# Grouped attention with a one-headed key beside an MLP: the output projection's products spread over a step, the first scores issued among the MLP's last products, and the row-sum test moved ahead of the last products

## The chip, the core and the metric

The kernel runs on one core of one Trainium2 chip. The metric is the device time of one execution in microseconds (us); of several runs the median is taken. Engines: TensorE (PE; its weight loads are PEld), VectorE (DVE), ScalarE (ACT), GpSimd (POOL) and SyncE (SP, which here only issues DMAs and waits). A queue of an engine that holds waits, branches and DMA issues carries a q behind the engine's name (SPq, PEldq).

## The reference

Input x has 2048 rows of 448. With xn = layernorm(x), the result is the sum of x, an attention and an MLP:

```
q = (xn @ wq) in 16 heads of 28;  k = xn @ wk;  v = xn @ wv      (one k and one v for all heads)
scores = q k^T * 28**-0.5;  p = softmax(scores);  attention = (p v, heads side by side) @ wo
h = gelu(layernorm(xn) @ w1 + b1);  mlp = h @ w2 + b2            (w1: 448 x 1792, w2: 1792 x 448)
out = x + attention + mlp
```

All is float32.

## The kernel before

The rows are cut into 4 chunks of 512. The program has four stages. The first normalizes x, transposes it and projects q, k and v; q goes to DRAM. The second is the MLP, in 56 slots (4 chunks by 14 column tiles of 128): `mlp1` multiplies by w1 (11 matmuls) and hands the result to ACT, DVE and POOL for the gelu and for a split in a high and a low part (`hh`, `hl`); `mlp2`, two slots later, multiplies both by w2 (12 matmuls) into four PSUM banks `m2`. After a chunk's last slot DVE adds the four banks to the rows (L596), which go back to DRAM. The last two `mlp2` slots stand by themselves, since no `mlp1` is left.

The third stage is attention, over 16 units (4 row chunks by 4 groups of 4 heads), unit u of 8 steps. A step issues 8 score matmuls (L700, for two key tiles and four heads), each into one of six PSUM banks; ACT turns each bank into weights by one exponential (L702). Behind the 8 scores stand the products of weights and values (`pv`, L709) for the scores of the step before, into the bank `po`; they are 8 in the program and 16 in the trace. The weights are not shifted by their true row maximum but by an estimate from a sample of the keys (`find_max`, once a unit: a matmul L536 into the bank `mo`, then DVE L537, L538, L542, L543). A column of ones in v gives the row sums. A fourth part, at the end, tests the row sums (`bad`, `count`): if one is outside of two limits, all of attention is done again with the true maximum. That code stands in the program behind a branch (L800) and is not run with these inputs.

Between the scores of a step stand side jobs of earlier units. Three matter here:

- `norm_jobs` of a finished unit: DVE copies `po` (L679), a DMA turns the row sums by 128 partitions (`rc`, L681), DVE stores them and takes the reciprocal (L683, L684), DMAs spread it through DRAM to all partitions (`tr`, L685, L688), DVE multiplies (L690) and splits (`oth` L692, `otl` L693 on POOL).
- `o_parts`: the output projection of a unit, four row tiles A to D, each with three matmuls (L665, L667, L669) that accumulate in `mo`, of which there is only one bank; after the third DVE adds `mo` to the row (L671). The first matmul of the next tile, and the matmul of `find_max`, wait until `mo` has been read.
- loads for the next unit (`load_unit`) and of rows for the next chunk.

A list `PIECES` says how many of the twelve matmuls stand in each of seven steps, 4 to 10 steps behind the end of the unit. Within a step the jobs stand at two places, after the second and after the fifth score; the list of a step's jobs is halved between them, in order of registration. So two matmuls of a step are neighbours where both fall in one half. After the last products `last_norm` (L712) normalizes the last unit, multiplies by wo (L719) and adds the rows (L732); then come the test (L792 to L798), the load of `count` into a register of each engine (L799) and the branch.

Of the kernel before, what the change touches and what calls it, by code (L numbers as in the profile page):

```python
# [10 lines left out]
F32 = mybir.dt.float32  # L11
# [7 lines left out]
P = 128  # L19
# [11 lines left out]
MLP_ORDER = 1, 2, 3, 0  # L31
HD = D // 2
WEIGHTS = 28
PIECES = 2, 1, 2, 1, 2, 2, 2
LIMITS = 0.25, 2.0 ** 40


# [1 line left out]
def block_kernel(ctx, tc, x, wq, wk, wv, wo, w1, b1, w2, b2, out):  # L39
# [511 lines left out]
    def find_max(u):  # L551
        mr = keep.tile([P, CW // 32], F32, name="mr", bufs=2)
        block_max(kd, mr)
        shift_rows(u, mr)

    ph1b = ExitStack()
    hp = ph1b.enter_context(tc.tile_pool(name="hp", bufs=3))
    php = ph1b.enter_context(tc.tile_pool(name="php", bufs=2, space=PSUM))
# [5 lines left out]

    def mlp1(c, ft):
        yh, yl = xts[MLP_ORDER[c], True]
        ph = php.tile([P, CW], F32, name="ph")
# [12 lines left out]
        pool.tensor_sub(hl, hx, f(hh))  # L580
        hs[c, ft] = (hh, hl)

    def mlp2(c, ft):
        if ft == 0:
            m2s[c] = [m2p.tile([P, CW], F32, name=f"m2_{k}")[:, 0:D] for k in range(CT)]
        m2 = m2s[c]
        hh, hl = hs.pop((c, ft))
        terms = ((hh, w2h), (hh, w2l), (hl, w2h))
        for k in range(CT):
            for i, (h, w) in enumerate(terms):  # L590
                pe.matmul(m2[k], h[:, k * P:(k + 1) * P], w[:, ft, :], start=(ft == 0 and i == 0),  # L591
                          stop=(ft == NF - 1 and i == 2))
            if ft == NF - 1:
                t = CT * MLP_ORDER[c] + k
                a = lines.pop(t)
                dve.tensor_add(a, a, m2[k])  # L596
                nc.sync.dma_start(ad[:, t, :], a)

    norms = {}
    mslots = [(c, ft) for c in range(NCH) for ft in range(NF)]  # L600
    for c in range(len(KEPT), NCH):
        g = norm_gen(MLP_ORDER[c], lambda shape: php.tile(shape, F32, name="ph"))
        for i in range(2 * CT + 1):
            norms[NF * (c - 1) + 4 + i] = lambda g=g: next(g, None)
    for n in range(len(mslots) + 2):
        c, ft = mslots[n] if n < len(mslots) else (NCH, n - len(mslots))
        if 3 <= ft < 11 and ft % 2 and len(KEPT) <= c + 1 < NCH:
            line(CT * MLP_ORDER[c + 1] + (ft - 3) // 2)
        k = ft - (10 if c < NCH - 1 else 5)
        if c < NCH and 0 <= k < CT:  # L610
            line(CT * MLP_ORDER[c] + k)
        if c < NCH and 0 < k <= CT:
            a = lines[CT * MLP_ORDER[c] + k - 1]
            pool.tensor_add(a, a, b2b)
# [12 lines left out]
        if n in norms:  # L627
            norms[n]()
        if (c, ft) == (NCH - 1, 7):
            find_max(0)  # L630
        if n >= 2:
# [5 lines left out]
    pr = ctx.enter_context(tc.tile_pool(name="pr", bufs=6, space=PSUM))  # L637
    op = ctx.enter_context(tc.tile_pool(name="op", bufs=1, space=PSUM))

    def weights_tile():  # L640
# [8 lines left out]
    dve.tensor_copy(woh, wor)  # L649
    dve.tensor_sub(wol, wor, f(woh))  # L650

    sums = keep.tile([P, NU, CW // 32], F32, name="sums")
    rows = {}
# [39 lines left out]
        pool.tensor_sub(otl, oc, f(oth))  # L693
        yield

    pos, ps = {}, {}

    def scores(u, kt, j):
        s = pr.tile([P, CW], F32, name="s")
        pe.matmul(s, ks[:, kt * P:(kt + 1) * P], qss[u][:, j, :], start=True, stop=True)  # L700
        p = att.tile([P, CW], F32, name="p", bufs=WEIGHTS)
        act.activation(p, s, AF.Exp, scale=SCALE)  # L702
        ps[u, kt, j] = p

    def pv(u, kt):
        if kt == 0:
# [2 lines left out]
            pe.matmul(pos[u][32 * j:32 * j + 32, :], vs[:, kt, :], ps[u, kt, j],  # L709
                      start=(kt == 0), stop=(kt == NT - 1))  # L710

    def last_norm(u, po):  # L712
# [3 lines left out]
        outs = [pr.tile([P, CW], F32, name="s") for _ in range(CT)]  # L716

        def product(k):
            pe.matmul(outs[k][:, 0:D], on[:, k * P:(k + 1) * P], wor[:, g, :], start=True, stop=True)  # L719

        for i in range(2):
            h, r = slice(256 * i, 256 * i + 256), slice(8 * i, 8 * i + 8)
            dve.transpose(tr[:, h], po[:, h])
            dve.reciprocal(rc[:, r], blocks(tr[:, h])[:, :, 0])
            dve.transpose(blocks(rb[:, h]), rc[:, r, None].to_broadcast([P, 8, 32]))
            dve.tensor_mul(on[:, h], po[:, h], rb[:, h])
            pool.tensor_copy(sums[:, u, r], blocks(tr[:, h])[:, :, 0])
            for k in (2 * i, 2 * i + 1):
                product(k)
        for k in range(CT):  # L730
            a = rows[c, k]
            dve.tensor_add(a, a, outs[k][:, 0:D])  # L732
            (nc.scalar if k % 2 else nc.sync).dma_start(ov[:, CT * c + k, :], a)

    side = {}

    def at(step, job):
        side.setdefault(min(step, PER * NU - 1), []).append(job)

    PER = NT // 2  # L740
    for u in range(NU):
# [6 lines left out]
    todo = [(u, kt, j) for u in range(NU) for kt in range(NT) for j in range(4)]  # L748
    waiting = []

    def weighted():
# [4 lines left out]
        norm = norm_jobs(u, pos.pop(u))  # L756
        next(norm)
        for d in (1, 3):
            at(PER * (u + 1) + d, lambda: next(norm))
        parts = []  # L760

        def part():
# [1 line left out]
                parts.append(o_parts(*units[u]))  # L764
            next(parts[0])

        for d, n in enumerate(PIECES if u < NU - 2 else (3, 3, 3, 3)):
            for _ in range(n):
                at(PER * (u + 1) + 4 + d, part)

    for step in range(PER * NU):
        for i in range(8):
            u, kt, j = todo.pop(0)
            scores(u, kt, j)
            if i in (1, 4):
                jobs = side.pop(step, [])
                if i == 1:
                    half = (len(jobs) + 1) // 2
                    side[step] = jobs[half:]
                    jobs = jobs[:half]  # L780
                for job in jobs:
                    job()
        weighted()
        waiting = [(u, kt - 1), (u, kt)]
    weighted()
    last_norm(NU - 1, pos.pop(NU - 1))

    bad = keep.tile([P, 2], F32, name="bad")
    count = keep.tile([1, 1], I32, name="count")
    bits = sums.rearrange("p u e -> p (u e)").bitcast(I32)  # L790
    lo, hi = (float(int.from_bytes(struct.pack(">f", v), "big")) for v in LIMITS)
    dve.tensor_reduce(bad[:, 0:1], bits, axis=AX.X, op=ALU.max)  # L792
    dve.tensor_reduce(bad[:, 1:2], bits, axis=AX.X, op=ALU.min)
    dve.tensor_scalar(bad[:, 0:1], bad[:, 0:1], hi, 0.0, op0=ALU.is_gt, op1=ALU.add)
    dve.scalar_tensor_tensor(bad[:, 0:1], bad[:, 1:2], lo, bad[:, 0:1], op0=ALU.is_lt, op1=ALU.add)
    pf = bank([1, 1])
    pe.matmul(pf, bad[:, 0:1], one[:, 0:1], start=True, stop=True)
    dve.tensor_copy(count, pf)  # L798
    outside = nc.values_load(count)  # L799
    with tc.If(outside > 0, preferred_fallthrough_block=False):  # L800
# [46 lines left out]
```

## Time and profile before

| what | value |
|---|---|
| three runs | 922.11, 922.5, 923.2 us; median 922.5 |
| the profiled execution | 923.97 us, of which the span from the first to the last instruction is 922.2 |
| granted TensorE clock, mean | 0.995 |
| PE / ACT / DVE busy | 97% / 73% / 32% of the span |
| MLP, first to last second-layer product | 76.5 to 351.8 us |
| attention, first score to last product of weights and values | 352.6 to 909.2 us |
| normalization of the last unit, test, branch, end | 909.2 to 922.2 us |

How it is read: the chain of waits follows back from the last instruction to what released it, and prints start, duration and what ran. A row of the groups or of the timeline gives in brackets, or behind a bar, the idle time of the engine before it and what ended that. Matmuls are pipelined: the next starts before the row of the last ends, so the chain's shares are better to count with than rows of single matmuls.

### The profile page before, as it was taken

What the parts mean: (1) busy time and instruction counts of PE and PEld (TensorE: products, weight loads), DVE (VectorE), ACT (ScalarE), POOL (GpSimd) and SP (SyncE); (2) the same over time, 40 slices, a digit from 0 to 9 for tenths busy, and PEclk for the clock granted to TensorE, in tenths of its full rate; (3) what the DMA queues carried; (4) which work ended last, traced back from release to release, by engine and by line L of the source; (5) the groups of instructions that cost most, each with busy time, mean ns of one, the idle gap of its engine ahead of it and who ended that gap; (6) DMA issues with size and microseconds to landing.
All of it is one profiled execution on the core that took longest, in us unless ns stands there. A gap on an engine that the chain in (4) does not pass through costs nothing.

```text
span 922.2 us, 13010 instructions
## 1 busy us (share of the span) xinstructions
PE 895.0 (97%) x4925; PEld 567.5 (62%) x4925; DVE 292.7 (32%) x551; ACT 676.4 (73%) x1284; POOL 155.4 (17%) x150
## 2 busy tenths in 40 slices
PE   9989999999999999999999999999999999999995
PEld 8867878888888885454454444444444454454442
DVE  7865454344444433012122122112122122121113
ACT  5754443334443337999999999999999999999983
POOL 6443243233234331000000000000000000000000
PEclk9999999999999999999999999999999999999998
DMA  9781112002003104302202312201312202222001
GB/s 298 207 270 40 41 61 80 1 1 80 21 21 96 28 9 125 92 23 63 42 22 53 96 58 55 49 23 53 101 53 53 52 23 53 84 70 53 1 13 44
DMA packets 42046, 60.08 MB, mean 65 GB/s; under 512 B 10794, under 2 KB 26744, under 8 KB 41976
## 3 DMA queue, kind: packets, MB, share of 16 engines
q1 hardware_dynamic: 40568, 58.60, 22.1%
q8 instruction: 41, 0.67, 0.3%
q10 hardware_dynamic: 1408, 0.57, 0.2%
q14 instruction: 29, 0.24, 0.1%
HBM read 43.16 MB, written 14.80 MB: 63 GB/s over the span
## 4 chain that ended last, share of the span: by engine, by line
PE 93%; DVE 3%; ACT 2%; issue 1%; POOL 0%; DMA 0%; ACTq 0%; DVEq 0%; POOLq 0%
PE s L700 29%; PE po L709 26%; PE m L591 14%; PE ph L177 12%; PE qp L177 3%; PE mo L665 2%; PE mo L669 1%; PE mo L667 1%; PE ph L182 1%; PE ph L180 1%; DVE row L671 1%; PE qp L301 1%; DVE hz L574 0%; PE mo L536 0%; DVE hx L576 0%
## 5 line engine op out<-in xcount | busy, mean ns | idle before, releaser
L702 ACT ACTIVATE p<-s 128x512 f32<-128x512 f32 x1024 | 516.0, 627 | 44.6 <-PE s L700 40.8
L700 PE MATMUL s<-xh,ks 128*128 128x512 f32 x1024 | 301.9, 408 | 0.8 <-issue 0.8
L700 PEld LDWEIGHTS s<-xh,ks 128*128 128x128 f32 x1024 | 182.5, 188 | 138.8 <-ACT p L702 110.3
L709 PE MATMUL po<-p,vs 128*32 128x512 f32 x2048 | 246.0, 598 | 0.0
L709 PEld LDWEIGHTS po<-p,vs 128*32 128x32 f32 x2048 | 53.5, 109 | 122.5 <-issue 117.0
L572 ACT ACTIVATE hx<-ph,b1t 128x512 f32<-128x512 f32 x56 | 38.5, 687 | 115.6 <-PE ph L182 105.9
L671 DVE TENSOR_TENSOR row<-row,mo 128x448 f32<-128x448 f32 x60 | 37.3, 621 | 244.8 <-PE mo L669 243.6
L580 POOL TENSOR_TENSOR hl<-hx,hh 128x512 fp32r<-128x512 f32 x56 | 77.5, 1384 | 184.4 <-DVE hh L579 181.7
L693 POOL TENSOR_TENSOR otl<-oc,oth 128x512 fp32r<-128x512 f32 x15 | 19.4, 1292 | 515.9 <-DVE oth L692 466.0
L591 PE MATMUL m<-w2l,hh 128*128 128x448 f32 x224 | 82.5, 369 | 0.9 <-DVE w2l L379 0.9
L591 PE MATMUL m<-w2h,hl 128*128 128x448 f32 x224 | 82.1, 367 | 1.0 <-POOL hl L580 1.0
L591 PE MATMUL m<-w2h,hh 128*128 128x448 f32 x224 | 82.3, 367 | 0.2 <-DVE a L596 0.2
L574 DVE SCALAR_TENSOR_TENSOR hz<-hz,hx 128x512 f32<-128x512 f32 x56 | 45.2, 808 | 106.0 <-ACT hz L573 105.7
L575 ACT ACTIVATE hz<-hz 128x512 f32<-128x512 f32 x56 | 35.4, 632 | 49.4 <-DVE hz L574 49.4
L177 PE MATMUL ph<-xh,w1h 128*128 128x512 f32 x168 | 66.1, 394 | 2.4 <-DVE qe L402 2.4
L177 PE MATMUL ph<-xl,w1h 128*128 128x512 f32 x168 | 66.3, 395 | 0.0
L177 PE MATMUL ph<-xh,w1l 128*128 128x512 f32 x168 | 66.2, 394 | 0.0
L576 DVE SCALAR_TENSOR_TENSOR hx<-hz,hx 128x512 f32<-128x512 f32 x56 | 39.1, 698 | 43.2 <-ACT hz L575 43.2
L679 DVE COPY oc<-po 128x512 f32<-128x512 f32 x15 | 10.4, 692 | 119.1 <-PE po L709 119.1
L591 PEld LDWEIGHTS m<-w2l,hh 128*128 128x128 f32 x224 | 42.1, 188 | 7.4 <-DVE w2l L379 3.3
L591 PEld LDWEIGHTS m<-w2h,hh 128*128 128x128 f32 x224 | 42.1, 188 | 5.5 <-DVE a L596 0.6
L591 PEld LDWEIGHTS m<-w2h,hl 128*128 128x128 f32 x224 | 42.1, 188 | 4.9 <-POOL hl L580 1.6
(148 smaller groups left out, 758.9 us busy)
## 6 DMA issues: line engine op xcount, KB each, us to landing
xh<-qd SPq DMA_DIRECT2D x64, 224.0 KB
qd<-qe SPq DMA_DIRECT2D x24, 256.0 KB
a<-in_A_x_dram SPq DMA_DIRECT2D x24, 224.0 KB
tr<-ld SPq DMA_DIRECT2D x60, 64.0 KB
ad<-a SPq DMA_DIRECT2D x16, 224.0 KB
qm<-qd SPq DMA_DIRECT2D x64, 56.0 KB
row<-ad SPq DMA_DIRECT2D x16, 224.0 KB
raw<-in_B_w_dram SPq DMA_DIRECT2D x7, 448.0 KB
```

Of the source, the lines that this page charges most:

```text
L177: pe.matmul(ps, w, v, start=(n == 0), stop=False)
L572: act.activation(hx, ph, AF.Identity, bias=b1t[:, ft:ft + 1])
L574: dve.scalar_tensor_tensor(hz, hz, 1.0, hx, op0=ALU.add, op1=ALU.mult)
L575: act.activation(hz, hz, AF.Tanh, scale=GELU[1])
L576: dve.scalar_tensor_tensor(hx, hz, 1.0, hx, op0=ALU.add, op1=ALU.mult)
L580: pool.tensor_sub(hl, hx, f(hh))
L591: pe.matmul(m2[k], h[:, k * P:(k + 1) * P], w[:, ft, :], start=(ft == 0 and i == 0), stop=(ft == NF - 1 and i == 2))
L671: dve.tensor_add(a, a, po)
L693: pool.tensor_sub(otl, oc, f(oth))
L700: pe.matmul(s, ks[:, kt * P:(kt + 1) * P], qss[u][:, j, :], start=True, stop=True)
L702: act.activation(p, s, AF.Exp, scale=SCALE)
L709: pe.matmul(pos[u][32 * j:32 * j + 32, :], vs[:, kt, :], ps[u, kt, j], start=(kt == 0), stop=(kt == NT - 1))
```

## The change

Five edits:

1. Side jobs get a slot of their own (`at(step, job, slot)`): the two or one matmuls of the output projection that a step holds stand after the second and the sixth score (three: also after the eighth), `norm_jobs` after the fourth, all else after the fifth. The counts of a step stay.
2. The six score banks are now two pools of three, `ring_a` and `ring_b`, used in turn. `ring_a` exists from the MLP on, whose `mlp1` uses it too (three banks in place of two). So in the MLP's last two slots `mlp2` issues one score after each three products, eight in all; their weights go into two free `xl` buffers. Step 0 then issues no scores.
3. The split of wo on DVE (`split_out`) moves from ahead of attention to step 3.
4. The row sums of the first 15 units are reduced ahead of the last products (`worst`); for the last unit the test stands inside `last_norm`, ahead of the reciprocal of the second half, and the two copies of sums on POOL go. One of the four last rows is added by ACT and POOL in place of DVE.
5. `mark_branch_hint_location("outside", hint="LikelyTaken")` stands ahead of `last_norm`, and the branch's preferred fallthrough is the code that does attention again, in place of the short block that skips it.

```
-PIECES = 2, 1, 2, 1, 2, 2, 2
+EARLY = 8
+PARTS = 2, 1, 2, 1, 2, 2, 2
...
+    ring_a = ctx.enter_context(tc.tile_pool(name="ra", bufs=3, space=PSUM))
...
+            if then is not None:
+                then()
...
+    def scores(u, kt, j):
+        s = score_bank()
+        pe.matmul(s, ks[:, kt * P:(kt + 1) * P], qss[u][:, j, :], start=True, stop=True)
+        p = early.pop(0) if early else att.tile([P, CW], F32, name="p", bufs=WEIGHTS)
+        act.activation(p, s, AF.Exp, scale=SCALE)
...
+        if n >= len(mslots):
+            t = f(xl_p.tile([P, 4, CW], F32R, name="xl"))
+            early.extend(t[:, k, :] for k in range(4))
+            mlp2(*mslots[n - 2], then=lambda: scores(*todo.pop(0)))
...
-        for i in range(2):
-            h, r = slice(256 * i, 256 * i + 256), slice(8 * i, 8 * i + 8)
+        for i, (h, r) in enumerate(halves):
             dve.transpose(tr[:, h], po[:, h])
+            if i == 1:
+                copy = flag(blocks(tr)[:, :, 0])
             dve.reciprocal(rc[:, r], blocks(tr[:, h])[:, :, 0])
             dve.transpose(blocks(rb[:, h]), rc[:, r, None].to_broadcast([P, 8, 32]))
+            if i == 1:
+                copy()
             dve.tensor_mul(on[:, h], po[:, h], rb[:, h])
-            pool.tensor_copy(sums[:, u, r], blocks(tr[:, h])[:, :, 0])
...
+            if k == 1:
+                act.activation(tr[:, 0:D], outs[k][:, 0:D], AF.Copy)
+                pool.tensor_add(a, a, tr[:, 0:D])
+            else:
+                dve.tensor_add(a, a, outs[k][:, 0:D])
...
         for d in (1, 3):
-            at(PER * (u + 1) + d, lambda: next(norm))
+            at(PER * (u + 1) + d, lambda: next(norm), 3)
...
+        for d, n in enumerate(PARTS if u < NU - 2 else (3, 3, 3, 3)):
+            for slot in (1, 5, 7)[:n]:
+                at(PER * (u + 1) + 4 + d, part, slot)
...
+    extremes(sums[:, 0:NU - 1, :].rearrange("p u e -> p (u e)").bitcast(I32), worst)
     weighted()
-    last_norm(NU - 1, pos.pop(NU - 1))
+    tc.mark_branch_hint_location("outside", hint="LikelyTaken")
+    last_norm(NU - 1, pos.pop(NU - 1), flag)
...
-    with tc.If(outside > 0, preferred_fallthrough_block=False):
+    with tc.If(outside > 0, preferred_fallthrough_block=True, label="outside"):
```

First place: PE in step 9 behind the end of a unit, the one step that holds the last matmul of tile C (L669, L698 after the change) and the first of tile D (L665, L694). Before:

```order
L700 MATMUL s<-xh,ks 128x512 x2
L669 MATMUL mo<-xl,otl 128x448
L665 MATMUL mo<-xl,oth 128x448
L700 MATMUL s<-xh,ks 128x512 x6
L709 MATMUL po<-p,vs 32x512 x8
```

and now (`s` and `t` are score banks of the two pools):

```order
L616 MATMUL s<-xh,ks 128x512
L616 MATMUL t<-xh,ks 128x512
L698 MATMUL mo<-xl,otl 128x448
L616 MATMUL s<-xh,ks 128x512
L616 MATMUL t<-xh,ks 128x512
L616 MATMUL s<-xh,ks 128x512
L616 MATMUL t<-xh,ks 128x512
L694 MATMUL mo<-xl,oth 128x448
L616 MATMUL s<-xh,ks 128x512
L616 MATMUL t<-xh,ks 128x512
L731 MATMUL po<-p,vs 32x512 x8
```

Four scores now stand between the two matmuls that share the bank `mo`.

Second place: DVE around step 11, where the second part of `norm_jobs` (L690, L692; L719, L721 after the change) meets `find_max` of the next unit (L537; L538 after the change). Before:

```order
L671 TENSOR_TENSOR row<-row,mo 128x448
L537 STREAM_TRANSPOSE tm<-mo 128x512
L538 TENSOR_REDUCE mr<-tm 128x16
L542 TENSOR_SCALAR mn<-mr 128x16
L543 STREAM_TRANSPOSE tm<-mn 128x512
L690 TENSOR_TENSOR oc<-oc,tr 128x512
L692 CAST oth<-oc 128x512
```

and now:

```order
L700 TENSOR_TENSOR row<-row,mo 128x448
L719 TENSOR_TENSOR oc<-oc,tr 128x512
L721 CAST oth<-oc 128x512
L538 STREAM_TRANSPOSE tm<-mo 128x512
L539 TENSOR_REDUCE mr<-tm 128x16
L543 TENSOR_SCALAR mn<-mr 128x16
L544 STREAM_TRANSPOSE tm<-mn 128x512
```

The multiplication that waits for the DMAs of `tr` now stands ahead of the transposition that frees `mo`.

Third place: PE at the end of the program. Before, with the short skipping block (the second branch) right behind the compare:

```order
L709 MATMUL po<-p,vs 32x512 x16
L719 MATMUL s<-xl,oc 128x448 x4
L797 MATMUL mo<-one,bad 1x1
L799 TENSOR_LOAD count
L800 COMPARE_AND_BRANCH
L800 UNCONDITIONAL_BRANCH
L536 MATMUL mo<-qm,ka 128x512 x64
```

and now:

```order
L731 MATMUL po<-p,vs 32x512 x16
L742 MATMUL s<-xl,oc 128x448
L742 MATMUL t<-xl,oc 128x448
L816 MATMUL mo<-one,bad 1x1
L742 MATMUL s<-xl,oc 128x448
L742 MATMUL t<-xl,oc 128x448
L835 TENSOR_LOAD count
L836 COMPARE_AND_BRANCH
L537 MATMUL mo<-qm,ka 128x512 x64
```

The test's matmul moved between the last four products, and behind the compare the repeated attention follows at once. No row stands for the announcement, on this engine or on another.

More of the change, by code (lines that the diff above doesn't have):

```diff
@@ L554, in find_max, with spare @@
         shift_rows(u, mr)
+    ring_a = ctx.enter_context(tc.tile_pool(name="ra", bufs=3, space=PSUM))
+    def spare():
+        return ring_a.tile([P, CW], F32, name="s")
     ph1b = ExitStack()
     hp = ph1b.enter_context(tc.tile_pool(name="hp", bufs=3))
-    php = ph1b.enter_context(tc.tile_pool(name="php", bufs=2, space=PSUM))
     m2p = ph1b.enter_context(tc.tile_pool(name="m2p", bufs=1, space=PSUM))
@@ L566, in mlp1 @@
         yh, yl = xts[MLP_ORDER[c], True]
-        ph = php.tile([P, CW], F32, name="ph")
+        ph = spare()
         fs = slice(ft * P, (ft + 1) * P)
@@ L581, in mlp1, with mlp2 @@
         hs[c, ft] = (hh, hl)
-    def mlp2(c, ft):
+    def mlp2(c, ft, then=None):
         if ft == 0:
@@ L597, in mlp2, with score_bank @@
                 nc.sync.dma_start(ad[:, t, :], a)
+            if then is not None:
+                then()
+    early = []
+    turn_s = itertools.count()
+    ring_b, ps = [], {}
+    todo = [(u, kt, j) for u in range(NU) for kt in range(NT) for j in range(4)]
+    def score_bank():
+        return ring_b[0].tile([P, CW], F32, name="t") if ring_b and next(turn_s) % 2 else spare()
+    def scores(u, kt, j):
[3 more added lines that the diff above has]
+        act.activation(p, s, AF.Exp, scale=SCALE)
+        ps[u, kt, j] = p
     norms = {}
@@ L601, in block_kernel @@
     for c in range(len(KEPT), NCH):
-        g = norm_gen(MLP_ORDER[c], lambda shape: php.tile(shape, F32, name="ph"))
+        g = norm_gen(MLP_ORDER[c], lambda shape: ring_a.tile(shape, F32, name="s"))
         for i in range(2 * CT + 1):
@@ L648, in block_kernel, with split_out @@
     woh, wol = weights_tile(), weights_tile()
-    dve.tensor_copy(woh, wor)
-    dve.tensor_sub(wol, wor, f(woh))
+    def split_out():
+        dve.tensor_copy(woh, wor)
+        dve.tensor_sub(wol, wor, f(woh))
     sums = keep.tile([P, NU, CW // 32], F32, name="sums")
@@ L694, in norm_jobs @@
         yield
[L696 to L703, printed above, removed]
+    pos = {}
     def pv(u, kt):
@@ L710, in pv, with last_norm @@
                       start=(kt == 0), stop=(kt == NT - 1))
-    def last_norm(u, po):
+    def last_norm(u, po, flag):
         c, g = units[u]
@@ L715, in last_norm @@
         rc = att.tile([P, CW // 32], F32, name="rc")
-        outs = [pr.tile([P, CW], F32, name="s") for _ in range(CT)]
+        outs = [score_bank() for _ in range(CT)]
+        halves = [(slice(256 * i, 256 * i + 256), slice(8 * i, 8 * i + 8)) for i in range(2)]
         def product(k):
             pe.matmul(outs[k][:, 0:D], on[:, k * P:(k + 1) * P], wor[:, g, :], start=True, stop=True)
-        for i in range(2):
-            h, r = slice(256 * i, 256 * i + 256), slice(8 * i, 8 * i + 8)
+        for i, (h, r) in enumerate(halves):
             dve.transpose(tr[:, h], po[:, h])
+            if i == 1:
+                copy = flag(blocks(tr)[:, :, 0])
             dve.reciprocal(rc[:, r], blocks(tr[:, h])[:, :, 0])
             dve.transpose(blocks(rb[:, h]), rc[:, r, None].to_broadcast([P, 8, 32]))
+            if i == 1:
+                copy()
             dve.tensor_mul(on[:, h], po[:, h], rb[:, h])
-            pool.tensor_copy(sums[:, u, r], blocks(tr[:, h])[:, :, 0])
             for k in (2 * i, 2 * i + 1):
@@ L731, in last_norm, with at @@
             a = rows[c, k]
-            dve.tensor_add(a, a, outs[k][:, 0:D])
+            if k == 1:
[3 more added lines that the diff above has]
+                dve.tensor_add(a, a, outs[k][:, 0:D])
             (nc.scalar if k % 2 else nc.sync).dma_start(ov[:, CT * c + k, :], a)
     side = {}
-    def at(step, job):
-        side.setdefault(min(step, PER * NU - 1), []).append(job)
+    def at(step, job, slot=4):
+        side.setdefault((min(step, PER * NU - 1), slot), []).append(job)
     PER = NT // 2
@@ L747, in block_kernel @@
             at(PER * (u + 1), lambda c=c: load_rows_of(c))
-    todo = [(u, kt, j) for u in range(NU) for kt in range(NT) for j in range(4)]
+    at(3, split_out)
     waiting = []
@@ L765, in part @@
             next(parts[0])
-        for d, n in enumerate(PIECES if u < NU - 2 else (3, 3, 3, 3)):
-            for _ in range(n):
-                at(PER * (u + 1) + 4 + d, part)
+        for d, n in enumerate(PARTS if u < NU - 2 else (3, 3, 3, 3)):
+            for slot in (1, 5, 7)[:n]:
+                at(PER * (u + 1) + 4 + d, part, slot)
+    bad = keep.tile([P, 2], F32, name="bad")
+    worst = keep.tile([P, 2], F32, name="worst")
+    count = keep.tile([1, 1], I32, name="count")
+    lo, hi = (float(int.from_bytes(struct.pack(">f", v), "big")) for v in LIMITS)
@@ new lines, in extremes, with flag @@
+    def extremes(src, to):
+        dve.tensor_reduce(to[:, 0:1], src, axis=AX.X, op=ALU.max)
+        dve.tensor_reduce(to[:, 1:2], src, axis=AX.X, op=ALU.min)
+    def flag(last):
+        extremes(last.bitcast(I32), bad)
+        dve.tensor_tensor(bad[:, 0:1], bad[:, 0:1], worst[:, 0:1], op=ALU.max)
+        dve.tensor_tensor(bad[:, 1:2], bad[:, 1:2], worst[:, 1:2], op=ALU.min)
+        dve.tensor_scalar(bad[:, 0:1], bad[:, 0:1], hi, 0.0, op0=ALU.is_gt, op1=ALU.add)
+        dve.scalar_tensor_tensor(bad[:, 0:1], bad[:, 1:2], lo, bad[:, 0:1], op0=ALU.is_lt, op1=ALU.add)
+        pf = bank([1, 1])
+        pe.matmul(pf, bad[:, 0:1], one[:, 0:1], start=True, stop=True)
+        return lambda: dve.tensor_copy(count, pf)
@@ L771, in block_kernel @@
+    done = EARLY
     for step in range(PER * NU):
         for i in range(8):
[L773 to L782, printed above, removed]
+            if done:
+                done -= 1
+            else:
+                scores(*todo.pop(0))
+            for job in side.pop((step, i), []):
+                job()
@@ L783, in block_kernel @@
         weighted()
-        waiting = [(u, kt - 1), (u, kt)]
+        waiting = [divmod(n, NT) for n in (2 * step, 2 * step + 1)]
+    extremes(sums[:, 0:NU - 1, :].rearrange("p u e -> p (u e)").bitcast(I32), worst)
     weighted()
-    last_norm(NU - 1, pos.pop(NU - 1))
[L788 to L798, printed above, removed]
+    tc.mark_branch_hint_location("outside", hint="LikelyTaken")
```

4 lines of the change are left out of this document (2 added, 2 removed).

## The prediction

> **What bounds the kernel now.** The page comes first: how long, and who is busy.
>
> ```profile
> span 922.2 us, 13010 instructions
> PE 895.0 (97%) x4925; PEld 567.5 (62%) x4925; DVE 292.7 (32%) x551; ACT 676.4 (73%) x1284; POOL 155.4 (17%) x150
> ```
>
> PE is busy nearly always, but two engines can bind in attention, so the busy time by stretch is next: the first ten steps, and one whole unit later on.
>
> ```profile
> 358.74:398.69 39.95, 39.95 (x247) 18.82 (x250) 7.85 (x11) 39.85 (x81) 0.00 (x0) 1.00 0.31 85
> 782.78:817.70 34.92, 34.21 (x210) 17.09 (x213) 6.89 (x14) 32.31 (x65) 1.29 (x1) 1.00 0.32 95
> ```
>
> Columns: length, busy PE, PEld, DVE, ACT, POOL, granted clock. While no unit has been finished there are no output products, and both PE (39.95 of 39.95) and ACT (39.85) are full. Later ACT rests 2.6 us in a unit and PE sets the pace. So in the first stretch both must start earlier for a gain; afterwards whatever PE loses counts in full. What PE waits for is in the waits (total, times, longest):
>
> ```profile
> PE mo L665 <- DVE row L671: 10.0, 14, 0.7
> ```
>
> Fourteen times, once a unit, the first matmul of a tile waits for DVE to empty `mo`. The chain of waits within that unit shows where (start, duration, what):
>
> ```profile
> 806.47 0.22 PE mo L669
> 806.68 0.02 issue
> 806.71 0.63 DVE row L671
> 807.34 0.04 issue
> 807.38 0.47 PE mo L665
> 807.86 1.41 PE s L700 x6
> ```
>
> **The change part by part.** *The projection's matmuls.* A product that waits for nothing costs 0.22 us (L669, 806.47). The L665 behind it makes the path from 806.68 to 807.86 last 1.18, so the stall costs 0.96: 0.70 of waiting, and 0.26 because the weights were loaded only after the wait. After the change four scores stand between; a score costs 1.41/6 = 0.235, so four take 0.94 of the 0.70 that DVE needs. The weight load of L694 goes ahead of its matmul by about one score: it is wanted at 806.68 + 0.94 - 0.23 = 807.39, and `mo` is free at 807.38. The two meet within 0.01, so I take 0.92, the filled hole less a hand-over, with 0.96 as the most and 0.70 as the least, if the load stays exposed. 14 x 0.92 = 12.9 us; bounds 9.8 and 13.4.
>
> Is there room for these scores, in banks and in ACT?
>
> ```profile
> 808.13 3.04 ACT L702 ACTIVATE p<-s 128x512 f32<-128x512 f32 x6 [0.77 <-PE s L700]
> ```
>
> In the very stall ACT runs dry for 0.77 us for want of a score, so the banks are free and the exponentials late, not early. A unit then takes PE 34.92 - 0.92 = 34.0 us. ACT needs 64 exponentials of 0.50 (38 in 19.00, below), 32.0: PE still binds.
>
> Here a rule of the Trainium skill can be set against the weight load, whose row is
>
> ```profile
> 807.38 0.19 PEld L665 LDWEIGHTS mo<-xl,oth 128*128 128x128 f32 x1 [1.11 <-DVE row L671]
> ```
>
> TensorE: Matmul & The Clock Gate, the table at its head, says that the engine's queue pulls weight loads ahead of matmuls in flight; by it the load would have been done during the wait, and the stall would cost 0.70 us, 9.8 in all. The trace does not agree here: the load starts only when DVE is done.
>
> *The order on DVE.* Putting the multiplication by `tr` ahead of the transposition that frees `mo` adds a wait: L538 and, behind it, the first product of the next step stand behind a DMA. Its traffic in 40 slices of 0.2 us, from 772 on in a usual unit and from 532 on in one where rows are loaded too:
>
> ```profile
> DMA  0000020000000012000000465446745100000000
> DMA  4333110004000000045025464559981000000000
> ```
>
> The first ends at 778.4, some 5 us before it is needed, so in usual units the multiplication runs early, in DVE's idle time, and costs nothing. The second ends at 538.2. What follows it on DVE, and when the product's weights were loaded before:
>
> ```profile
> 537.01 0.72 DVE L537 STREAM_TRANSPOSE tm<-mo 128x512 f32<-128x512 f32 x1 [2.82 <-PE mo L536]
> ...
> 539.33 0.65 DVE L690 TENSOR_TENSOR oc<-oc,tr 128x512 f32<-128x512 f32 x1
> 540.01 0.43 DVE L692 CAST oth<-oc 128x512 fp32r<-128x512 f32 x1
> ```
>
> ```profile
> 540.49 0.19 PEld L665 LDWEIGHTS mo<-xl,oth 128*128 128x128 f32 x1
> ```
>
> Now `mo` is free at 538.2 + 0.65 + 0.43 + 0.72 + 0.1 = 540.1, while PE, 0.92 earlier, wants it at 539.57: a stall of 0.5 to 0.8 us. Units 4 and 12 are so; unit 8, the third with row loads, I count with a little. I charge 1.2 us; bounds 0 and 3 x 0.8 = 2.4.
>
> *The first scores.* The chain around the end of the MLP:
>
> ```profile
> 339.02 2.43 PE m L591 x12
> ...
> 343.74 0.24 PE ph L182
> ...
> 349.55 2.29 PE m L591 x10
> 351.84 0.76 issue
> 352.60 6.14 PE s L700 x16
> 358.74 1.85 PE po L709 x16
> ```
>
> ```profile
> 350.06 2.44 DVE L596 TENSOR_TENSOR a<-a,m 128x448 f32<-128x448 f32 x4 [2.02 <-PE m L591]
> 353.19 19.00 ACT L702 ACTIVATE p<-s 128x512 f32<-128x512 f32 x38 [6.47 <-PE s L700]
> ```
>
> Three second-layer slots of 2.43 follow 343.98; they end at 351.84, not 351.27, as the last slot waits for `hl`. Then PE waits 0.76 until DVE has added the last bank (350.06 + 2.44 = 352.50). Then 16 scores take 6.14, at ACT's pace. Afterwards: 343.98 + 3 x 2.43 + 8 x 0.235 = 353.15, the wait for `hl` covered by four scores (0.94 against 0.57). In step 1 the second score takes a bank of the added ones, free at 353.15 - 0.24 + 0.62 + 0.04 = 353.57, so some 0.25 is lost; eight scores with one exposed weight load (0.2) take 2.1. The products of weights and values start at 355.5 in place of 358.74: 3.2 us. On ACT, exponential 8 starts at about 353.7, before at 353.19 + 8 x 0.50 = 357.19: 3.5. Both engines are full in the stretch that follows, so the smaller counts: 3.3 us taken between them, bounds 2.5 and 3.6. The wo split leaves a free DVE queue for a place behind `find_max`, with nothing waiting behind it until the unit's end: nothing.
>
> *The end.* From the last product of weights and values on, and the branch's rows from the view by line (count, shortest/median/longest ns, first and last start):
>
> ```profile
> 910.93 3.31 PE s L719 x8
> ...
> 914.88 0.33 DVE bad L792
> ...
> 916.08 0.15 DVE count L798
> ```
>
> ```profile
> L799 PEldq TENSOR_LOAD <-count x1: 485/485/485, 916.3 to 916.3; - x1
> L800 PEldq COMPARE_BRANCH  x2: 95/2102/4110, 916.9 to 917.2; - x2
> L800 SPq COMPARE_BRANCH  x2: 38/46/53, 916.8 to 917.5; - x2
> L843 SPq EVENT_SEMAPHORE  x10: 17/28/28, 920.4 to 922.1; - x10
> ```
>
> The first compare costs 95 ns; the jump over the repeated attention costs PE 4.11 us (917.2 to 921.3) and SP 2.9 (917.5 to 920.4). What runs after 921.3 is 0.9. Today every engine waits for `count` at 916.23, behind the last row's addition (done at 914.88). Afterwards the test's six small DVE operations (0.15 each by `count`, 0.33 at most by L792: 0.9, bound 2) and the copy of 0.15 stand ahead of the second half's product. So the last product ends 1.0 later, at 914.24 + 1.0 = 915.2, and the last row is added by 915.9; but `count` needs only the test's matmul, which runs behind the first half's products (910.93 + 3.31/2 = 912.6), so it is ready by 913.1 and nobody waits for it. PE takes 0.5 for its register behind its last product and has jumped by 915.2 + 0.5 + 0.1 + 4.1 = 919.9. SP issues its last row ahead of the last addition, by 915.6, has its register at 916.1, and the jump and its 16 waits (0.6 for eight, 916.9 to 917.5) end at 916.1 + 0.1 + 2.9 + 1.1 = 920.2. So the last engine comes at 920.2 in place of 921.3: 1.1 us. The taken compare's own cost isn't in the trace; I take that of the jump, the row of the same distance. If it cost nothing, 2.9 more would go; if all engines waited for the last add, 0.3 would be lost. The announcement puts no instruction in any engine's order, so I give it nothing. The Trainium skill's page Runtime: NRT & Kernel Launch, Instruction fetch mechanics, says that a taken branch out of the fetched window waits for its target; by it the compare pays as the jump did, which no row of this trace shows.
>
> *Sum*: -12.9 + 1.2 - 3.3 - 1.1 = -16.1 us. The profiled execution took 923.97, 1.5 above the median of the runs, 922.5; it becomes 907.9, and the median 906.4.
>
> **The rivals.**
> *DVE's queue takes the stall back (slower).* If `tr` lands late in every unit, PE stalls at each unit's first product. Against it is the first DMA row: only units with row loads land late. The point from which it decides: a usual unit's product wants its weights at 540.49 + 7 x 34.92 - 0.92 = 784.0, DVE needs 1.9 from landing to free `mo`, and the landing is at 778.4, so 3.7 are to spare. The other gains are 12.9 + 3.3 + 1.1 = 17.3, which 1.24 of stall in each of 14 units would eat: landings 4.9 later than now. At 5.5 later the stall is 1.8 and the time 922.5 - 17.3 + 25.2 = 930. Slower: 4 in 100.
> *Half of the stall stays.* If `mo` is freed later than worked out in most units (a DVE still busy with the copy L679, a late landing), the load is exposed again and half of the first term goes: 906.4 + 6.4 = 913. 13 in 100.
> *The jump goes too.* If the compare does not pay the fetch, 2.9 more: 903.5. 5 in 100.
> *It does nothing*: the scores moved into the hole only meet another wait, and ACT starts early to no end: 922.5. For it speaks that both engines are full at 358 to 398; against it, that both start earlier. 2 in 100.
>
> **How the numbers follow.** The forecast as worked has 76 in 100; its bounds add up to between -9.8 + 2.4 - 2.5 + 0.3 = -9.6 and -13.4 - 3.6 - 1.1 - 2.9 = -21.0, hardly all at once. The range that holds 8 in 10 leaves out the worst corners: 902 to 912. A change under 0.2%, 1.8 us, cannot be told from none. Faster by more: 0.76 + 0.13 + 0.05 = 0.94; same 0.02; slower 0.04.
>
> **What would show it.** Right: no wait of L694 on L700 of 0.7 us in the waits (only some short ones on L538, in units 4 and 12); units of 34.0 us; first products of weights and values near 355.5, ACT without a rest before them; PE's taken compare of 4 us starting near 915.8, with `count` long there. Wrong: L694 waiting in most units, the waits `DMA tr` on DVE with PE idle behind, a unit of over 34.5, or a jump that starts after 916.5.

## The result, and the profile after

| | before | after |
|---|---|---|
| median of the runs, same chip | 922.85 us (922.11 to 923.86, 4 runs) | 907.68 us (905.49 to 909.06, 4 runs) |
| profiled execution, its span | 923.97, 922.2 us | 906.6, 904.8 us |

The ratio is 0.9833, 95% interval 0.9808 to 0.9858. The forecast was 906.4 with a range of 902 to 912; the change is faster. A second sample of the kernel after (`after_again`, below) gave 908.65 and a ratio of 0.9848 (0.9833 to 0.9864), so the gain is 13.5 to 15.2 us on the medians. The two profiles differ by 17.4, because that of before was 1.1 above its median here and that of after 1.1 below. Of the four runs after, the two with a mean granted clock of 0.992 took 908.76 and 909.06, those with 0.997 and 0.999 took 906.6 and 905.49.

The page of the kernel after, and its busy time in the two stretches that were shown of before:

```profile
span 904.8 us, 13015 instructions
...
PE 889.1 (98%) x4925; PEld 567.7 (63%) x4925; DVE 293.7 (32%) x554; ACT 676.6 (75%) x1285; POOL 156.4 (17%) x149
```

```profile
355.20:394.69 39.49, 39.49 (x242) 18.70 (x242) 7.74 (x12) 39.23 (x80) 0.35 (x1) 1.00 0.43 109
771.00:804.99 33.99, 33.99 (x206) 17.12 (x206) 5.23 (x10) 32.22 (x65) 0.34 (x1) 1.00 0.33 97
```

A unit takes 33.99 us in place of 34.92, and PE is busy for all of it (before: 34.21 of 34.92). PE still sets the pace; ACT rests 1.8 us. The waits of the kernel after no longer have a row of PE for `mo`, only the weight load's, which other matmuls cover:

```profile
PEld mo L694 <- DVE row L700: 3.1, 14, 0.2
```

The thirteen units between the copies of `po` of the second and the fifteenth unit, from the timeline of DVE, took 454.02 us before (421.77 to 875.79) and take 441.89 now:

```profile
418.24 0.69 DVE L708 COPY oc<-po 128x512 f32<-128x512 f32 x1 [6.97 <-PE po L731]
...
860.13 0.69 DVE L708 COPY oc<-po 128x512 f32<-128x512 f32 x1 [7.04 <-PE po L731]
```

The chain at the end of the MLP, to be held against the one of before:

```profile
343.43 0.23 PE s L183
343.66 3.05 PE m L596 x15
...
352.62 0.63 DVE a L601
...
353.30 0.51 PE t L616
...
355.20 1.85 PE po L731 x16
```

The last first-layer matmul ends at 343.66 and the first product of weights and values starts at 355.20, 11.54 later; before, these were 343.98 and 358.74, 14.76 apart. So the difference by stage is: up to this matmul -0.3, early scores and banks -3.2, thirteen units -12.1, the last unit -0.9, and the rest, from the last product of weights and values to the end (13.15 before, 12.34 now), -0.8. Together -17.4, the difference of the spans.

The end, by line: first the load of the register, then the branch (the columns are those of before):

```profile
L835 PEldq TENSOR_LOAD <-count x1: 491/491/491, 896.8 to 896.8; - x1
...
L835 ACTq TENSOR_LOAD <-count x1: 477/477/477, 900.6 to 900.6; - x1
```

```profile
L836 SPq EVENT_SEMAPHORE  x8: 17/17/17, 902.4 to 903.4; - x8
...
L836 PEldq COMPARE_BRANCH  x1: 4162/4162/4162, 897.4 to 897.4; - x1
...
L836 SPq COMPARE_BRANCH  x1: 50/50/50, 899.6 to 899.6; - x1
L836 ACTq COMPARE_BRANCH  x1: 58/58/58, 901.1 to 901.1; - x1
...
L836 ACTq EVENT_SEMAPHORE  x1: 17/17/17, 903.9 to 903.9; - x1
```

PE's taken compare costs 4.16 us, about what the jump cost before (4.11), and it starts earlier. The exact size varies: in the other profiles with this end and without a named announcement it takes 3.4 to 4.3. PE is through at 901.6. The engines that come last are others. ACT issues the last row, loads its register at 900.6, compares at 901.1, and has its next instruction at 903.9, 2.7 later; SP's waits begin 2.8 after its compare and end about as late.

### The profile page after: what moved, and what is told of

Same layout as the page of the kernel before. It is cut to its first block, busy times and chain, and to the rows that moved or that the text cites. A ratio compares the mean times of both kernels' runs of the same rounds, so it can differ in the third digit from the quotient of the medians.

```text
span 904.8 us, 13015 instructions
## 1 busy us (share of the span) xinstructions
PE 889.1 (98%) x4925; PEld 567.7 (63%) x4925; DVE 293.7 (32%) x554; ACT 676.6 (75%) x1285; POOL 156.4 (17%) x149
## 4 chain that ended last, share of the span: by engine, by line
PE 94%; DVE 2%; ACT 1%; issue 0%; DMA 0%; POOL 0%; ACTq 0%; DVEq 0%; POOLq 0%
PE po L731 26%; PE s L616 16%; PE m L596 14%; PE t L616 13%; PE s L178 12%; PE qp L178 3%; PE mo L694 1%; PE mo L696 1%; PE mo L698 1%; PE s L181 1%; PE s L183 1%; PE qp L302 0%; DVE hz L579 0%; PE mo L537 0%; PE qp L181 0%
## 5 line engine op out<-in xcount | busy, mean ns | idle before, releaser
L618 ACT ACTIVATE p<-s 128x512 f32<-128x512 f32 x508 | 315.5, 621 | 26.7 <-PE s L616 22.3
L618 ACT ACTIVATE p<-t 128x512 f32<-128x512 f32 x508 | 319.5, 629 | 0.0
L616 PE MATMUL s<-xh,ks 128*128 128x512 f32 x516 | 216.6, 420 | 0.0
L616 PE MATMUL t<-xh,ks 128*128 128x512 f32 x508 | 200.4, 394 | 0.3 <-DVE a L601 0.3
L616 PEld LDWEIGHTS s<-xh,ks 128*128 128x128 f32 x516 | 97.0, 188 | 121.6 <-ACT p L618 105.6
L577 ACT ACTIVATE hx<-s,b1t 128x512 f32<-128x512 f32 x56 | 38.5, 688 | 115.3 <-PE s L183 105.6
L616 PEld LDWEIGHTS t<-xh,ks 128*128 128x128 f32 x508 | 95.5, 188 | 14.0 <-ACT p L618 1.9
L178 PE MATMUL s<-xh,w1h 128*128 128x512 f32 x168 | 66.1, 394 | 2.4 <-DVE qe L403 2.4
L178 PE MATMUL s<-xh,w1l 128*128 128x512 f32 x168 | 66.3, 395 | 0.0
L178 PE MATMUL s<-xl,w1h 128*128 128x512 f32 x168 | 66.3, 395 | 0.0
```

What stands on the lines that cost most here:

```text
L178: pe.matmul(ps, w, v, start=(n == 0), stop=False)
```

## The experiments

Each kernel is the kernel after with the edit shown. The kernels of one batch ran on the same chip beside the kernel before (median 922.78, 922.28 and 922.13 in the three batches). Nearly all of the work is the same in them, so a profile is read by its stages.

The first stage has to be paired with care. Near 63.5 PE waits 2.4 us for DVE in each of the 14 profiles. Around 66 the granted clock falls to 0.50 in seven of them (before, after, adjacent, late_tr, late_tr_fm, hint_spin, best) and not in the other seven. Here are 60 to 70 us of after, then of spin (the seventh figure is the clock):

```profile
60.00:70.00 10.00, 7.56 (x28) 5.56 (x27) 4.17 (x8) 2.63 (x4) 2.27 (x2) 0.83 0.81 278
60.00:70.00 10.00, 7.57 (x35) 5.69 (x34) 4.17 (x8) 3.89 (x6) 2.26 (x2) 1.00 0.86 295
```

A mean of 0.83 over 10 us is 3.4 us at 0.50. Where it falls, the last first-layer matmul ends at 343.3 to 343.7 in the changed kernels, and where it does not, at 342.0 to 342.2; the three kernels with the announcement of hint are left out here. The profiles before and after both have the fall, so their stages can be compared.

**adjacent.** The stall put back.

```
-            for slot in (1, 5, 7)[:n]:
+            for slot in (1, 1, 7)[:n]:
```

> Only the slots differ from the kernel after: two matmuls of the projection in a step are neighbours again, so the last of tile C (L698) and the first of tile D (L694) stand side by side. Theory (the stall was the waiting for `mo` plus an exposed weight load): L694 waits on L700 about 14 times by 0.7 us, the unit grows from 33.99 to 34.92 us, and the time from 907.7 by 14 x 0.94 = 13.2 to about 921. Rival (the gain came from the earlier start and the end, the slots moved nothing): unit 34.0, time 908.

Measured: 921.53 us, ratio 0.9989 (0.9977 to 1.0). Its waits, and the copies of `po` as above:

```profile
PEld mo L694 <- DVE row L700: 15.7, 14, 1.1
...
PE mo L694 <- DVE row L700: 10.0, 14, 0.7
```

```profile
417.99 0.69 DVE L708 COPY oc<-po 128x512 f32<-128x512 f32 x1 [7.00 <-PE po L731]
...
873.03 0.69 DVE L708 COPY oc<-po 128x512 f32<-128x512 f32 x1 [7.06 <-PE po L731]
```

455.04 / 13 = 35.00 us a unit, 1.01 more than after. The 10.0 us in 14 waits are those of the kernel before to the tenth. Against the kernel after the median grows by 13.9, so the slots carry most of the gain, and the rival falls. What is left of the gain is 3.4 us between the spans of the profiles (918.8 against 922.2), but only 1.3 between the medians; six of the ten runs of adjacent had a mean clock of 0.992 to 0.995.

**gap2.** Two scores between, in place of four: what does the weight load cost?

```
-            for slot in (1, 5, 7)[:n]:
+            for slot in (1, 3, 7)[:n]:
```

> As the kernel after, but the second matmul of a step stands after the fourth score in place of the sixth: two scores (0.47 us) between L698 and L694, not four. Theory (the load of the weights waits with its matmul): of 0.70 of waiting and 0.26 of exposed load 0.96 - 0.47 = 0.49 stays in a unit, unit 34.45, 14 x 0.47 = 6.6 more, time 914.3. Rival one (the weights are loaded during the wait): only 0.70 - 0.47 = 0.23 stays, 3.2 more, time 911. Rival two (any score between is enough): 908.

Measured: 913.74 us, ratio 0.9912 (0.9886 to 0.9937).

```profile
PEld mo L694 <- DVE row L700: 9.6, 14, 0.7
...
PE mo L694 <- DVE row L700: 3.5, 14, 0.3
```

```profile
416.74 0.69 DVE L708 COPY oc<-po 128x512 f32<-128x512 f32 x1 [6.98 <-PE po L731]
...
865.09 0.69 DVE L708 COPY oc<-po 128x512 f32<-128x512 f32 x1 [7.04 <-PE po L731]
```

The wait of PE is 3.5 / 14 = 0.25, as 0.70 less two scores leaves. But the unit is 448.35 / 13 = 34.49, 0.50 more than after, so 0.25 more are lost that no wait of the matmul shows: the weight load of 0.19 and its hand-over. From none over two to four scores a unit falls by 0.51 and 0.50. So where the matmul had to wait for another engine, its load waited with it, and this cost about 0.25 a time. The rule of the Trainium skill that the prediction weighed (TensorE: Matmul & The Clock Gate, the table at its head, that weight loads are pulled ahead of matmuls in flight) did not show for such a load. The trace agrees with it where nothing is waited for: in the kernel after a load of L694 starts at 669.16, 0.23 ahead of its matmul and while a score runs.

**late_tr.** The prediction's slower rival made real: `tr` is issued behind the addition of tile D.

```
-        for d in (1, 3):
-            at(PER * (u + 1) + d, lambda: next(norm), 3)
+        for d, slot in ((2, 6), (3, 3)):
+            at(PER * (u + 1) + d, lambda: next(norm), slot)
```

> As the kernel after, but the reciprocal of the row sums stands behind the last addition of step 2, so `tr` is issued and lands about 4.3 us later in a usual unit. It tests the rival of the prediction in which DVE's queue holds `mo`. Theory: the multiplication L719 then starts at about 12.3 behind the copy of `po` in place of 8.06, the transposition L538 behind it frees `mo` 1.2 later than PE wants it for L694, unit 35.2, 14 x 1.2 = 17 more, time 925. Rival (PE does not wait for this transposition, its wait is elsewhere): 908 to 909.

Measured: 928.05 us, ratio 1.0061 (1.0042 to 1.0081), slower than the kernel before. One usual unit on DVE, and the wait in all:

```profile
743.27 0.17 DVE L712 COPY sums<-rc 128x16 f32<-128x16 f32 x1
...
748.68 0.69 DVE L719 TENSOR_TENSOR oc<-oc,tr 128x512 f32<-128x512 f32 x1 [4.95 <-DMA tr<-ld]
749.40 0.43 DVE L721 CAST oth<-oc 128x512 fp32r<-128x512 f32 x1
749.75 0.71 DVE L538 STREAM_TRANSPOSE tm<-mo 128x512 f32<-128x512 f32 x1
```

```profile
PE mo L694 <- DVE tm L538: 13.9, 13, 2.1
```

So the mechanism is real: with the multiplication queued ahead of the transposition, a `tr` that is some 4.2 us later (the multiplication starts 12.20 behind the copy of `po`, against 8.06) makes this change a loss. The usual unit loses 0.96 (34.95), less than the 1.2 worked out; in several units `tr` lands about 1 us later still, and the thirteen units average 35.34, so the sum is more than expected.

**late_tr_fm.** The same, with the transposition ahead of the multiplication.

```
+        for d, slot in ((2, 6), (3, 5)):
```

> As late_tr, but the transposition of find_max (L538) stands ahead of the multiplication by `tr` (L719) on DVE, as it did in the kernel before. Theory: `mo` is free early, and PE waits only for `oth` itself, ready 0.6 later than wanted: unit 34.6, 14 x 0.6 = 8.4 more, time 916. Rival (the landing alone sets the stall, the order on DVE does not matter): as late_tr, 925.

Measured: 921.17 us, ratio 0.9975 (0.9962 to 0.9988): the order is worth 7 us here, so the rival falls, but 5 more are lost than expected: in five units `tr` lands later still and they take 35.1 to 35.9, and in this profile the last stage took 2.0 longer than after, at a clock of 0.50. The usual unit takes 34.57, and PE waits for `oth`, as expected; but it is not the late landing that makes `oth` late, as `best` shows below.

**no_early.** No scores in the MLP's last slots.

```
-EARLY = 8
+EARLY = 0
...
-        if n >= len(mslots):
-            t = f(xl_p.tile([P, 4, CW], F32R, name="xl"))
-            early.extend(t[:, k, :] for k in range(4))
-            mlp2(*mslots[n - 2], then=lambda: scores(*todo.pop(0)))
-        elif n >= 2:
+        if n >= 2:
```

> As the kernel after, but no score is issued within the MLP's last two slots; step 0 of attention issues its eight. Theory (both engines are full in the first stretch and started earlier together): the first product of weights and values moves from 355.2 back to about 358.7, every unit keeps its 33.99, and the time goes from 907.7 to 911.2. Rival (later waits give the early start back): 907.7 to 908.5.

Measured: 908.09 us, ratio 0.9849 (0.9835 to 0.9862). This lies between the two samples of the kernel after, so the medians don't resolve it. At a mean clock of 0.999 three of its runs took 907.8 to 908.09 and one of the kernel after took 905.49, some 2.4 less. The chain shows where:

```profile
341.96 0.24 PE s L183
...
350.11 0.63 DVE a L601
...
350.79 0.50 PE t L616
...
356.38 1.85 PE po L727 x16
```

From the last first-layer matmul (342.20) to the first product of weights and values it takes 14.18: 2.64 more than after, 0.58 less than before. So the early scores bring 2.6, and 0.6 of the 3.2 come from the other edits at this place (the third bank for the MLP, the split of wo moved); which of these wasn't separated. The 2.6 are not given back behind: the units take 33.99 as in the kernel after, but for one of 34.71 (unit 12, below). From the last first-layer matmul to the end this profile is 3.0 longer than that of the kernel after, and its first stage, where the clock did not fall, was 1.5 shorter.

**old_tail.** The end of the kernel before in the kernel after.

```
-    tc.mark_branch_hint_location("outside", hint="LikelyTaken")
-    last_norm(NU - 1, pos.pop(NU - 1), flag)
+    last_norm(NU - 1, pos.pop(NU - 1))
+    flag()
...
-    with tc.If(outside > 0, preferred_fallthrough_block=True, label="outside"):
+    with tc.If(outside > 0, preferred_fallthrough_block=False):
```

> As the kernel after, but with the end of the kernel before: the test behind the last additions, all four additions on DVE, the copies of the sums on POOL, and the short skipping block right behind the compare. Theory: from the last product of weights and values to the end 13.05 us as before in place of 12.34, time 908.4. Rival (the end's saving was larger and the early test hides the branch's fetch): over 909.5.

Measured: 907.61 us, ratio 0.9839 (0.9823 to 0.9854). Inconclusive: no difference that the runs resolve. In its profile the last stage took 14.78, but PE's clock fell to 0.65 there, so it can't be held against 12.34.

**hint and hint_reg.** Is there anything to be had from an announcement that becomes an instruction?

```
-    tc.mark_branch_hint_location("outside", hint="LikelyTaken")
+    tc.mark_branch_hint_location("outside", hint="LikelyTaken", engines=(mybir.EngineType.PE, mybir.EngineType.SP, mybir.EngineType.DVE, mybir.EngineType.Activation, mybir.EngineType.Pool))
```

In hint_reg, `hint=nc.values_load(zero)` stands in place of the constant.

> As the kernel after, but the announcement names the five engines, so that each really gets an instruction for it; the compiler puts it at the head of each engine's program, some 900 us ahead of the branch. Theory (it is too early, other fetches follow): nothing changes, PE's compare 4.16 us, 907.7. Rival (it stays armed until the branch): PE's compare under 0.2 us, SP and ACT go on at once instead of 2.8 us after their compares, the end at 902.1 of the span in place of 904.8, time 905.

> As the kernel after, but the announcement stands on each of the five engines where the last products of weights and values are issued; its outcome comes from a register that is loaded there from a zero. Theory (the block at the end is then fetched ahead): PE's compare under 0.2 us, SP and ACT without the 2.8 us behind theirs, the last engine done at 902.1 of the span or before, 2.7 us less: 905. Rival (the announcement does nothing): 907.7, or up to 0.5 more for the register loads.

Measured: hint 906.61 us, ratio 0.9831 (0.9818 to 0.9845); hint_reg 906.27 us, 0.983 (0.9816 to 0.9845). The branch's rows of hint:

```profile
L836 SPq EVENT_SEMAPHORE  x8: 17/17/17, 901.0 to 903.4; - x8
...
L836 PEldq COMPARE_BRANCH  x1: 403/403/403, 897.5 to 897.5; - x1
...
L836 SPq COMPARE_BRANCH  x1: 70/70/70, 900.4 to 900.4; - x1
...
L836 ACTq COMPARE_BRANCH  x1: 76/76/76, 901.9 to 901.9; - x1
L836 ACTq EVENT_SEMAPHORE  x1: 17/17/17, 902.3 to 902.3; - x1
```

For hint the rival holds on the engines: PE's compare costs 0.40 in place of 4.16, SP goes on after 0.5 and ACT after 0.4, though the announcement stood 900 us ahead. In hint_reg only PE profits (0.49); SP still takes 2.9 and ACT 2.6. Why the nearer announcement does less stays open. And yet the time hardly moves: SP's last waits end at 903.4 as before. They are for the last output row: its transfer ends at 902.67 in hint, and at 902.81 in the kernel after. What was hidden behind the fetch, a DMA's landing, is the next thing late. This pair of profiles is not a clean one: in that of hint the clock fell to 0.50 ahead of the last products, and the addition of the last row started at 900.25, against 898.62. In spin and hint_spin below, both at 1.00 there, the last stage differs by 0.25. Besides, in the profiles of hint, hint_spin and best the last first-layer matmul ends at 343.01, 344.20 and 344.33, which is 0.5 to 1.0 later than in the others with the same clock in the first stage. So the announcement seems to lose ahead of attention what it gains at the end; why stays open.

**after_again, spin, hint_spin, best.** Profiles of the last stage differed by up to 2.8 us, with the granted clock. The last batch runs the kernel after again, then with six matmuls that keep PE busy behind the last products (spin), with these and hint's announcement (hint_spin), and with `find_max` ahead besides (best).

```
     weighted()
+    warmth = bank([P, P])
+    for _ in range(6):
+        pe.matmul(warmth, ident, ident, start=True, stop=True)
...
-            at(PER * (u + 1) + d, lambda: next(norm), 3)
+            at(PER * (u + 1) + d, lambda: next(norm), 2 + d)
```

(The last two lines are in best only.)

> The kernel after once more, unchanged, as the measure for the three beside it. Theory: 907 (905.5 to 909), ratio 0.983; the normalization of unit 12 or 4 may wait up to 0.7 us for `tr` in some executions. From the last addition of a row to the end 5.5 us (5.56 in the first profile): ACT's compare waits 2.7 for its code, and SP's last wait stands until the last row has been written.

> As the kernel after, with six matmuls of the unit matrix, whose result nobody reads, behind the last products of weights and values, in PE's gap of 1.9 us. The granted clock fell to 0.5 in the last stage of the profiles of hint, old_tail and late_tr_fm, and the stage took 12.8 to 14.8 us there in place of 12.3. Theory (the gap lets the clock fall): the clock is 1.00 in the last stage of every profile, 0.5 to 1 us off the median, 906.8. Rival (the clock falls for another reason, or the matmuls delay the last products): no change or slower, 907.7.

> The announcement at the head of each engine's program, as in hint, and the six matmuls of spin. Theory: with the clock at 1.00, the last addition comes 6.8 behind the last product of weights and values as in the kernel after, and from there to the end it takes 3.9 as in hint in place of 5.56: 1.6 us less than after, 906 or below. Rival (the landing of the last row sets the end, whatever is announced): 907.5.

> As hint_spin, and the transposition of find_max stands ahead of the multiplication by `tr` on DVE again, as in the kernel before, with `tr` issued as early as in the kernel after. Theory: all 13 units at 33.99, no unit of 34.2 to 34.7 at row loads, 0 to 0.7 us less than hint_spin: 905.5. Rival (the order of these two on DVE costs nothing where `tr` is early, and the splitting is later): as hint_spin or 0.5 more.

Measured: after_again 908.65 us, ratio 0.9848 (0.9833 to 0.9864); spin 905.88, 0.9829 (0.9809 to 0.985); hint_spin 906.65, 0.9823 (0.981 to 0.9837); best 914.86, 0.9915 (0.9902 to 0.9929). Busy time by stretch of after_again and of spin, from the last product of weights and values on (the seventh figure is the clock):

```profile
891.53:895.00 3.47, 1.57 (x4) 0.83 (x4) 3.05 (x13) 0.00 (x0) 0.00 (x0) 0.86 0.00 0
895.00:899.00 4.00, 3.43 (x7) 1.26 (x6) 1.33 (x5) 0.54 (x1) 1.14 (x1) 0.50 0.18 64
```

```profile
890.71:894.00 3.29, 2.93 (x16) 2.02 (x16) 2.87 (x13) 0.00 (x0) 0.00 (x0) 1.00 0.00 0
894.00:897.50 3.50, 2.26 (x7) 0.76 (x6) 2.53 (x6) 0.54 (x1) 1.13 (x1) 1.00 0.29 107
```

The last stage took 15.12 us in after_again, 11.87 in spin and 11.62 in hint_spin. The clock fell ahead of the last product in 4 of the 10 profiles of changed kernels without the six matmuls, and in none of the 3 with them. The mean clock, which is on record for every run, says more: in this batch it was 0.991 to 0.995 in the four runs of after_again, and 0.996 to 0.999 in all fifteen with the six matmuls. This speaks for the matmuls holding the clock up. That they save time is not shown: the runs of spin took 904.46 to 909.52, those of after_again 907.8 to 909.23. hint_spin has the lowest ratio; its interval ends at 0.9837 where that of after_again begins at 0.9833, so it is probably faster than the kernel after too, by some 2 us.

best is 8 us slower than hint_spin, against expectation. DVE in one unit of it, and the waits:

```profile
740.80 0.72 DVE L538 STREAM_TRANSPOSE tm<-mo 128x512 f32<-128x512 f32 x1 [3.28 <-PE mo L537]
...
742.48 0.71 DVE L544 STREAM_TRANSPOSE tm<-mn 128x512 f32<-128x512 f32 x1
743.12 0.65 DVE L719 TENSOR_TENSOR oc<-oc,tr 128x512 f32<-128x512 f32 x1
743.80 0.43 DVE L721 CAST oth<-oc 128x512 fp32r<-128x512 f32 x1
```

```profile
PEld mo L694 <- DVE oth L721: 10.2, 14, 0.7
...
PE mo L694 <- DVE oth L721: 4.1, 14, 0.3
```

`tr` landed early (738.2), but the multiplication now stands behind the four operations of `find_max`, `oth` is ready at 744.23, and PE wants the product some 0.6 earlier: units of 34.57. In the usual units of late_tr_fm the multiplication stands 12.47 behind the copy of `po`, as it does here, so their 34.57 come from the order and not from the landing. With `find_max` as late in its step as the change puts it, the multiplication has to go ahead; that order is part of the gain and no free side effect.

## Why the prediction was right, point by point

*The stall (-12.9).* Right in place, mechanism and size. Over thirteen units the gain is 12.1, and 0.9 in the last. The stall itself measured 1.01 with neighbours (0.96 worked out), and four scores take it to where PE has no gap left. The exposed weight load, which the prediction kept, is borne out by gap2.

*The order on DVE (+1.2).* The term that failed. In the profile after, the units 4 and 12 take 33.99 like the others. Here is unit 12 of the kernel after, then of hint_spin:

```profile
792.16 0.69 DVE L708 COPY oc<-po 128x512 f32<-128x512 f32 x1 [7.04 <-PE po L731]
...
797.80 0.17 DVE L712 COPY sums<-rc 128x16 f32<-128x16 f32 x1 [4.25 <-DMA rc<-oc]
...
803.33 0.69 DVE L719 TENSOR_TENSOR oc<-oc,tr 128x512 f32<-128x512 f32 x1 [4.30 <-DMA tr<-ld]
```

```profile
799.28 0.17 DVE L712 COPY sums<-rc 128x16 f32<-128x16 f32 x1 [5.26 <-DMA rc<-oc]
...
804.74 0.69 DVE L719 TENSOR_TENSOR oc<-oc,tr 128x512 f32<-128x512 f32 x1 [4.52 <-DMA tr<-ld]
```

In hint_spin the copy of `po` starts at 792.63; so the row sums are there 6.65 behind it against 5.64, and the multiplication 0.94 later. That unit takes 34.87, against 33.99. The prediction carried the landing over from the old profile (538.2, 11.6 behind the copy of `po`); `tr` now is there 11.0 behind in unit 4 and 11.2 in unit 12, and the product just makes it. Over the profiles with the order and slots of the change, unit 4 never loses, and unit 12 loses between 0 and 0.9. So the price is 0 to 0.9 and not 1.2; the bounds held. The prediction also saw only a cost in this order: `best` shows that with the old order and the new slots the change is 8 us slower.

*The first scores (-3.3).* 3.2 measured between the same two events, the first product at 355.20 against 355.5 forecast. About 2.6 of it are the early scores themselves.

*The end (-1.1).* 0.8 in the two profiles with the clock at 1.00; the runs can't resolve it. The path that it had last, SP, came as worked out: its compare stands 7.0 behind the last product of weights and values in the chain (forecast 7.0), its last wait 10.8 (forecast 11.0). "PE takes 0.5 for its register behind its last product" was wrong, as the load runs while the last products do (896.8), so PE is done early; it is not on the path, so this changed nothing. What the prediction left out is ACT: its issue of the last row, its register and its branch end 11.3 behind that product, after SP. That is the 0.3 missing.

*The sum.* Without the 0.3 up to the last first-layer matmul the profiles give -17.1 where -16.1 was forecast, since the 1.2 was not paid. The medians give -15.2 and, with the second sample, -13.5. No term stood for the clock, whose mean was 0.991 to 0.995 in six of the eight runs of the kernel after and 0.997 and 0.999 in the others. So the forecast of 906.4 lies near 907.68 in part by luck: a cost that was not paid stands against one that was not foreseen.

*The rivals.* That DVE's queue takes the stall back did not happen, and late_tr shows how near it is. The jump does not go: 4.16 us, and 3.4 at the least in the profiles without a named announcement. The announcement as written gave nothing, as forecast; the compare paid as the jump did, in line with what the prediction cited from the Trainium skill's page Runtime: NRT & Kernel Launch.

## What to carry to other kernels

Where an accumulator bank is read by another engine between two matmuls, put work between them that is as long as the reading plus the weight load behind it, and count what that pulls earlier: here the next product came 0.9 us earlier too, and only holds because the operation that feeds it was put ahead on DVE. Before an operation that waits for a DMA is queued ahead of one that frees a bank, read how far ahead its landing is in each kind of unit. At the end of a program list every engine's last wait, the landing of the output among them, before crediting a faster branch.

## What the runs showed of the hardware that was not expected

- An announcement with the engines named, 900 us ahead of the branch, cut PE's taken compare from 4.16 to 0.40 us (0.50 in hint_spin and best) and the wait behind SP's and ACT's from 2.8 and 2.7 to 0.5 and 0.4.
- PE's register load (896.8, 0.49 long) ran beside its last products, which ended at 898.6.
- The clock fell to 0.50 in the last stage of some profiles, where the longest wait of PE is 1.9 us, and in half of all profiles around the end of the wait of 2.4 us near 63.5; in the three profiles with the last gap filled it stayed at 1.00 up to the last product. The stretch at 0.50 near 66 lasted 3.4 us. The Trainium skill's page TensorE: Matmul & The Clock Gate, Part 1, has the clock fall after an idle window of about 3.4 us that runs on its own, which would explain why only some runs are hit. Both waits here are shorter than that window, and no run shows what counts as idle within it.
- Profiles with and without the fall near 66 differ by 1.1 to 1.7 us up to the last first-layer matmul, with no edit there; this hides effects of 1 us in whole times.
